# A decode step of gated attention and MLP: wo's extra rows loaded as one block, the biases of w1 and w2 applied elsewhere

## The chip, the cores and the metric

The kernel runs on one core of a Trainium2 chip. The metric is device time in microseconds (us) of one execution. A core has five engines that run in parallel: TensorE (PE; its weight loads are shown as PEld), VectorE (DVE), ScalarE (ACT), GpSimd (POOL) and SyncE (SP), which here issues nearly all loads. The loads themselves are carried out by 16 DMA engines, which work in parallel with all of these.

## What is computed

One token x (576 numbers, bf16) goes through two branches, and a gate mixes them:

```
g = sigmoid(sum(x * gate_w))
# branch a: attention of 32 query heads over 16 key/value heads,
#           the last 4096 positions of a cache, head size 128
q = x @ wq                                  # wq: 576 x 4096
p = softmax(q k^T / sqrt(128));  o = p v    # k, v: 16 x 4096 x 128 each
a = o @ wo                                  # wo: 4096 x 576
# branch b: MLP with a tanh gelu
b = gelu(x @ w1 + b1) @ w2 + b2             # w1: 576 x 4608, w2: 4608 x 576
out = g * a + (1 - g) * b
```

All inputs are bf16. About 53.6 MB must be read, 33.6 of them keys and values.

## The kernel before

**Stages.** SP issues the loads in one order: w1 (L234), wq (L238), the keys in four groups of four heads (L554, `k_t`), two groups of values, a third one, two small loads of wo (L670), the last group of values, the main part of wo (L771), the first half of w2 (L775) and the second half in four pieces of 10, 5, 2 and 1 rows per partition (L777). Big tiles share four buffers, named by the tags A to D: key group 2 goes where w1 was, group 3 where wq was, the values where keys were, wo and w2 last. A load therefore waits on SP until the last reader of its buffer is done. The small rows (x, the gate's weights, b2, b1) are loaded on ACT's queue at the start (L226 to L229).

**h stage.** x is put into a 32-column weight (`x2`). The function `moved` (L404) multiplies it with the nine rows per partition of w1: it takes the pieces four at a time, each of the four into another quarter of the output's partitions, and goes over five outputs (four of 512 columns, `h_m` of 256). Of the nine pieces, four and four fill two rounds. The ninth makes a third round together with b1, which is multiplied as two rows with a 2x32 corner of the identity, in the next quarter. A later product (L441) adds the four quarters up. A pass over the built program (`keep_weights`, L95) drops a weight load if the same weights still stand in that place and no weights of another size have been loaded between. ACT, POOL and DVE turn h into `gt`, the gelu with the factor (1 - g).

**q and attention.** wq is multiplied in the same way (L500). Then, by groups of four heads, DVE transposes the keys (L566), PE makes the scores (L588), DVE takes maxima, ACT exponentials, DVE transposes the probabilities, and PE multiplies them with the values (L681). A function `queue` keeps the instructions of an engine in the written order.

**Output stage.** wo has 128 rows for each of the 32 heads. The first 124 of a head are cut into 4 parts of 31 rows; the 32 x 4 parts fill the 128 partitions of `wo_t`. The four rows left of each head (124 to 127) are the extra rows, `wo_tail`: 32 heads, each 4 x 576 bf16 = 4,608 bytes. They lie in a part of the tile `zeros`, heads 0 to 15 in partitions 0 to 15 and heads 16 to 31 in partitions 32 to 47, and are loaded by two DMAs of 16 rows. A pass over the built program (`split_outer`, L74) gives each of these loads an outer dimension of 4:

```
ins=[copy.replace(src, ap=[[n // k * step, k], [step, n // k], [1, size]])],
outs=[copy.replace(dst, ap=[[part, n], [1, 1], [1, size]])],
```

The result y is accumulated in PSUM: `y_add` (L385) makes two products of 288 columns, the two halves of y, into partition 0 and partition 32 of `y_ps`. The first of these, L398, starts the sum early, with the row b2 x (1 - g) (`b2g`, L376) times 32 ones, so that partitions 0 to 31 and 32 to 63 all hold something. After attention come the four tail products (`ov_tail` times `wo_tail`), the 31 products with `wo_t`, and the first 23 rows of w2. A few fp32 products into a spare bank stand between (L831). DVE then copies `y_ps` to SBUF (`y_kept`, L844). The last 13 rows of w2 go into another pair of sums (`end_a`, `end_b`, L851); after the fifth of them, `y_carry` (L863) adds `y_kept` to these with a weight that picks rows 0 and 32. ACT and DVE cast the two parts (L879, L880), and SP stores them (L881).

The functions that the change touches:

Of the kernel before, what the change touches and what calls it, by code (L numbers as in the profile page):

```python
# [9 lines left out]
FP32 = mybir.dt.float32  # L10
BF16 = mybir.dt.bfloat16
I32 = mybir.dt.int32
ACT = mybir.ActivationFunctionType
ALU = mybir.AluOpType
# [4 lines left out]
def kernel(  # L19
# [15 lines left out]
    nc = tc.nc  # L35

    P = 128
    D = 576
    Hq, Hkv, Dh = 32, 16, 128
# [12 lines left out]
    DH = D // 2  # L52
# [19 lines left out]
    few_engines = {}  # L72
# [138 lines left out]
    const = ctx.enter_context(tc.tile_pool(name="const", bufs=1))  # L211
# [10 lines left out]
    b2_row = rows[0:1, 2 * D : 3 * D]  # L222
    b1_t = rows[0:2, 3 * D : 3 * D + FH]
# [21 lines left out]
    for base, pattern, keep in (  # L245
# [6 lines left out]
        n = 1  # L252
# [8 lines left out]
        out=is0[:], in0=low[:], scalar1=0.0, scalar2=None, op0=ALU.is_equal  # L261
    )
    alt = is0[:, 0 : 2 * NI].rearrange("p (i t) -> p i t", t=2)
    ones = const.tile([P, P], FP32, name="ones")
    nc.gpsimd.memset(ones[:], 1.0)
    ident = const.tile([P, P], BF16, name="ident")
    make_identity(nc, ident[:])
    RW = 31
    NZ = 5 * RW + 1 + 64
    ROWS = NZ + 4 * D  # L270
    zeros = const.tile([P, ROWS + 32 * HB], BF16, name="zeros")
    nc.gpsimd.memset(zeros[:].bitcast(FP32), 0.0)
    at31 = zeros[:, 0 : 5 * RW].rearrange("p (a r) -> p a r", a=5)
    om_t = zeros[:, NZ - 64 : NZ]
    wo_tail = zeros[0:48, NZ : NZ + 4 * D].rearrange("p (j n) -> p j n", j=4)
    nc.gpsimd.affine_select(
        out=at31,
        in_=at31,
# [8 lines left out]
        out=hi5[:],  # L287
        in_=ones[:, 0:5],
# [7 lines left out]
        out=hi5[:],  # L296
        in_=hi5[:],
# [9 lines left out]
        out=hi16[:], in0=is0[:, c0 : c0 + 16], scalar1=-SCALE, scalar2=None, op0=ALU.mult  # L307
# [6 lines left out]
        out=row_of,  # L314
        in_=row_of,
# [9 lines left out]
        out=foreign[:],  # L325
        in_=foreign[:],
# [11 lines left out]
        out=xdup.rearrange("p (d t) -> p d t", t=2),  # L338
        in_=x_row.rearrange("p (d o) -> p d o", o=1).to_broadcast([1, D, 2]),
    )  # L340
    xs_ps = ps_m.tile([P, NI, 1], FP32, name="xs_ps", tag="m")
    for i in range(NI):
        nc.tensor.matmul(  # L343
            xs_ps[:, i, :],
            lhsT=xdup[:, i : 2 * D : NI],
            rhs=ident[0:1, 0:1],
            start=(i == 0),
            stop=(i == NI - 1),
# [3 lines left out]
        out=x2[:, :, 0:2], in0=xs_ps[:].to_broadcast([P, NI, 2]), in1=alt, op=ALU.mult  # L352
# [5 lines left out]
        out=junk_row,  # L358
        in0=x_row,
        in1=gw_row,  # L360
        scale=1.0,
# [11 lines left out]
    nc.vector.reciprocal(out=g_t[:], in_=ge[:])  # L373
    omg = const.tile([P, 1], FP32, name="omg")
    nc.scalar.activation(out=omg[:], in_=g_t[:], func=ACT.Copy, scale=-1.0, bias=1.0)
    b2g = const.tile([1, D], FP32, name="b2g")  # L376
    nc.scalar.activation(out=b2g[:], in_=b2_row, func=ACT.Copy, scale=omg[0:1, 0:1])
    gh = const.tile([P, 1, 5], FP32, name="gh")
    nc.scalar.activation(out=gh[:, 0, :], in_=hi5[:], func=ACT.Copy, scale=g_t[:, 0:1])

# [1 line left out]
    y_ps = ps_y.tile([64, DH], FP32, name="y_ps")  # L382
    end_b = ps_y.tile([64, DH - DA], FP32, name="end_b")

    def y_add(vec, row, start=False, stop=False):  # L385
        wide = vec.shape[-1]
        for s in range(2):
            last = nc.tensor.matmul(  # L388
                y_ps[32 * s : 32 * s + wide, :],
                lhsT=vec,  # L390
                rhs=row[:, DH * s : DH * s + DH],
                start=start,
                stop=stop,
                skip_group_check=True,
            )
        return last

    y_add(ones[0:1, 0:32], b2g[0:1, :], start=True)  # L398


    QZ = 24
# [2 lines left out]
    def moved(pieces, last, start):  # L404
        for g0 in range(0, len(pieces), 4):
            for n in range(len(last)):
                for g in range(min(4, len(pieces) - g0)):
                    vec, part = pieces[g0 + g]
                    nc.tensor.matmul(  # L409
                        last[n][32 * g : 32 * g + 32],  # L410
                        lhsT=vec,
                        rhs=part(n),
                        start=start and g0 == 0,
                        stop=g0 + 4 + g >= len(pieces),
                        skip_group_check=True,
                    )
# [3 lines left out]
    h_out = [h_s[q // 2][:, 512 * (q % 2) : 512 * (q % 2) + 512] for q in range(4)]  # L420
    h_out.append(h_m[:])

    def columns(row):
        rows4 = row.rearrange("p (q l j) -> p q l j", q=4, j=NJ)
        return lambda n: rows4[:, n, :, 0:16] if n < 4 else rows4[:, :, :, 16:NJ]

    steps = [(x2[:, i, :], columns(w1_t[:, i, :])) for i in range(NI)]
    moved(steps[:4], h_out, True)
    moved(steps[4:] + [(ident[0:2, 0:32], columns(b1_t))], h_out, False)

    turned = kt_pool.tile([P, 2 * 1024 + 256], FP32, name="turned", tag="kt")
    for c0, src, q in ((0, h_s[0], 2), (1024, h_s[1], 2), (2048, h_m, 4)):
        n = 1024 if q == 2 else 256
        nc.vector.transpose(  # L434
            out=turned[:, c0 : c0 + n],
            in_=src[:].rearrange("p (q l j) -> p q j l", q=q, l=32),
# [3 lines left out]
    for j0, j1, b0 in ((0, 16, 0), (16, NJ, 64)):  # L440
        nc.tensor.matmul(  # L441
            hp_ps[:, :, :, j0:j1].rearrange("p q t j -> p q j t"),
            lhsT=same32,
            rhs=turned_t[:, b0 : b0 + 4 * (j1 - j0), :],
            start=(j0 == 0),
            stop=True,
# [3 lines left out]
    for q in range(4):  # L450
        quad = slice(32 * q, 32 * q + 32)
        nc.scalar.copy(
            out=hacc[quad], in_=hp_ps[quad, q, :, :].rearrange("p t j -> p (t j)")
# [6 lines left out]
        out=poly[:],  # L460
        in0=z2[:],
# [14 lines left out]
        out=gt[:], in0=hacc[:], scalar=omg[:, 0:1], in1=r_t[:], op0=ALU.mult, op1=ALU.mult  # L476
# [7 lines left out]
        out=pick[:],  # L484
        in_=pick[:],
# [16 lines left out]
    for c in range(2):  # L502
        nc.vector.transpose(  # L503
            out=q_turned[:, 1024 * c : 1024 * c + 1024],
            in_=q_s[c][:].rearrange("p (h l b) -> p h b l", l=32, b=2),
# [4 lines left out]
        lhsT=same32,  # L510
        rhs=q_turned[:].rearrange("p (h j l) -> p h j l", h=16, j=4)[:, :, :, 0:2],
        start=True,
        stop=True,
    )
    for b in range(4):
        quad = slice(32 * b, 32 * b + 32)
        at = QZ + 32 * b
# [4 lines left out]
            out=diag[:, :, :, 0:8],  # L522
            in_=qj_ps[quad].rearrange("p j g q -> p g j q"),
# [15 lines left out]
    o_ps = mt_ps[:, NG * 16 + Hq : NG * 16 + 2 * Hq]  # L539
    issued = {}  # L540

    def queue(engine, emit):
        if engine in issued:
            with tc.issue_after(issued[engine].ins):
                issued[engine] = emit()
        else:
            issued[engine] = emit()
# [117 lines left out]
    v_t = [load("v_t", "CD"[g], A_v_cache, g) for g in range(2)]  # L665
    v_t.append(load("v_t", "A", A_v_cache, 2))
    wo_src = A_wo.rearrange("(h d) n -> h d n", d=P)
    tail = wo_src[:, 4 * RW : P, :]
    for h0, h1, at, k in ((0, 16, 0, 4), (16, Hq, 32, 4)):
        load_tail = nc.sync.dma_start(  # L670
            out=wo_tail[at : at + h1 - h0].rearrange("h j n -> h (j n)"),
            in_=tail[h0:h1].rearrange("h j n -> h (j n)"),
        )
        few_engines[load_tail.ins.name] = k
    acc = [None] * NG
    summed = [None] * NG
    free_banks = []
# [35 lines left out]
    def outputs(g):  # L713
# [19 lines left out]
        out=ls[:],  # L733
        in0=same8[:, 0:8].rearrange("p (o q) -> p o q", o=1).to_broadcast([P, NG, 8]),
        in1=sums[:].to_broadcast([P, NG, 8]),
        op=ALU.mult,
# [11 lines left out]
            t_ps, lhsT=ones[:], rhs=ls[:].rearrange("p g q -> p (g q)"), start=True, stop=True  # L748
# [5 lines left out]
    rgh = const.tile([P, Hq, 5], FP32, name="rgh")  # L754
    nc.gpsimd.tensor_tensor(
        out=rgh[:],
        in0=rg[:].to_broadcast([P, Hq, 5]),
        in1=gh[:].to_broadcast([P, Hq, 5]),
        op=ALU.mult,
# [9 lines left out]
    RO = RW  # L769
    wo_t = big.tile([P, RO, D], BF16, name="wo_t", tag="D")  # L770
    nc.sync.dma_start(  # L771
        out=wo_t[:].rearrange("p r n -> p (r n)"),
        in_=wo_src[:, 0 : 4 * RW, :].rearrange("h (a r) n -> h a (r n)", a=4),
    )
    nc.sync.dma_start(out=w2_t[:, 0:NJ, :], in_=w2_src[:, 0])  # L775
    for j0, j1 in ((0, 10), (10, 15), (15, 17), (17, 18)):
# [5 lines left out]
    queue(  # L782
        "dve",
        lambda: nc.vector.tensor_tensor(
            out=om_t.rearrange("p (u h) -> p u h", u=2)[:, :, 0:16],
            in0=o_ps.rearrange("p (u h) -> p u h", u=2),
            in1=rgh[:, :, 4].rearrange("p (u h) -> p u h", u=2),
            op=ALU.mult,
        ),
    )  # L790
    queue(
# [2 lines left out]
            out=om[:], in0=o_all.to_broadcast([P, Hq, 4]), in1=rgh[:, :, 0:4], op=ALU.mult  # L794
# [3 lines left out]
    queue(  # L798
        "pe",
        lambda: nc.tensor.matmul(  # L800
            ov_ps[0:64, RO : RO + 4], lhsT=om_t, rhs=at31[:, 4, 0:4], start=True, stop=True
        ),
    )
    for a in range(4):
# [9 lines left out]
        )  # L814
    ov = const.tile([P, RO], BF16, name="ov")
    nc.vector.tensor_copy(out=ov[:], in_=ov_ps[:, 0:RO])
    ov_tail = const.tile([48, 4], BF16, name="ov_tail")
    nc.scalar.copy(out=ov_tail[:], in_=ov_ps[0:48, RO : RO + 4])

    late = [(ov_tail, j, wo_tail[:, j, :]) for j in range(4)]  # L820
    late += [512]
# [5 lines left out]
    for n, item in enumerate(late):  # L827
        if isinstance(item, int):
            queue(
                "pe",  # L830
                lambda: nc.tensor.matmul(  # L831
                    spare[:, 0:item],
                    lhsT=ones[:],
                    rhs=p_t[:].rearrange("p c k -> p (c k)").bitcast(FP32)[:, 0:item],
                    start=True,
                    stop=True,
                ),
            )
            continue
        vec, at, row = item  # L840
        queue("pe", lambda: y_add(vec[:, at : at + 1], row))

    y_kept = kt_pool.tile([33, DH], FP32, name="y_kept", tag="kt")
    nc.vector.tensor_copy(out=y_kept[:], in_=y_ps[0:33, :])  # L844
    end_a = ps_m.tile([64, DA], FP32, name="end_a", tag="m")
    ends = ((0, DA, end_a[0:2, :]), (DA, DH, end_b[32:34, :]))

# [64 lines left out]
```

## Time and profile before

| | us |
|---|---|
| median of three runs | 131.16 (130.96 to 131.59) |
| profiled execution | 131.3 |
| its span, first to last instruction | 130.0 |
| PE busy / share of the span | 79.6 / 61% |
| DVE busy / share | 61.3 / 47% |
| ACT, POOL busy | 11.4, 10.5 |
| chain that ended last: share of DMA, DVE, PE | 61%, 21%, 10% |
| bytes read from HBM, mean rate | 53.62 MB, 412 GB/s |

The page of the profile divides the span into 40 slices and gives each engine's busy share in tenths; the row DMA is the mean share of the 16 DMA engines. The chain that ended last is followed back from the last instruction, at each step to what released it. A timeline shows start and length of each instruction, with the tile it writes, the tiles it reads, and in brackets how long its engine was idle before it and what ended that. Besides, the trace holds one record for each DMA packet: queue, start, duration and size. A packet is one contiguous row of a load; packets of 4 bytes are the semaphore writes with which each DMA engine ends its share of a load.

### The profile page before, as it was taken

What the parts mean: (1) busy time and instruction counts of PE and PEld (TensorE: products, weight loads), DVE (VectorE), ACT (ScalarE), POOL (GpSimd) and SP (SyncE); (2) the same over time, 40 slices, a digit from 0 to 9 for tenths busy, and PEclk for the clock granted to TensorE, in tenths of its full rate; (3) what the DMA queues carried; (4) which work ended last, traced back from release to release, by engine and by line L of the source; (5) the groups of instructions that cost most, each with busy time, mean ns of one, the idle gap of its engine ahead of it and who ended that gap; (6) DMA issues with size and microseconds to landing.
All of it is one profiled execution on the core that took longest, in us unless ns stands there. A gap on an engine that the chain in (4) does not pass through costs nothing.

```text
span 130.0 us, 1210 instructions
## 1 busy us (share of the span) xinstructions
PE 79.6 (61%) x572; PEld 26.1 (20%) x442; DVE 61.3 (47%) x51; ACT 11.4 (9%) x27; POOL 10.5 (8%) x36
## 2 busy tenths in 40 slices
PE   0001499495007994859949945993374064789985
PEld 0001202200001120201212201140222021326553
DVE  0003104417099669999999994357705005100010
ACT  2130300210300000030003003012000000000000
POOL 7005940010000000000000000000100000000000
PEclk9999999959555899977999999599559558658999
DMA  8999899899899899799799899999999998999980
GB/s 255 499 460 421 364 420 488 353 474 474 353 464 474 338 474 474 333 484 484 343 464 484 373 433 484 403 403 479 378 433 444 427 461 373 459 394 427 412 328 29
DMA packets 2362, 53.69 MB, mean 413 GB/s; under 512 B 271, under 2 KB 404, under 8 KB 694
## 3 DMA queue, kind: packets, MB, share of 16 engines
q1 hardware_dynamic: 2348, 53.61, 96.6%
q8 instruction: 4, 0.07, 0.2%
q10 hardware_dynamic: 10, 0.01, 0.0%
HBM read 53.62 MB, written 0.00 MB: 412 GB/s over the span
## 4 chain that ended last, share of the span: by engine, by line
DMA 61%; DVE 21%; PE 10%; issue 5%; SPq 2%; DVEq 0%
DMA k_t<-in_A_k_cache_dram 34%; DMA w_t<-in_B_w_dram 26%; DVE kt L566 15%; PE s_ps L588 4%; DVE m L604 3%; DVE pt L637 2%; PE s_ps L681 1%; PE acc L681 1%; PE end_a L851 1%; SPq L775 1%; PE y_ps L388 1%; PE end_b L851 1%; PE mt_ps L613 1%; DVE mr L607 1%; SPq L554 0%
## 5 line engine op out<-in xcount | busy, mean ns | idle before, releaser
L588 PE MATMUL s_ps<-kt,qz_flat 128*128 128x512 bf16 x128 | 33.8, 423 | 13.1 <-DVE kt L566 9.4
L566 DVE STREAM_TRANSPOSE kt<-k_t 128x4096 f32<-128x4096 f32 x8 | 35.3, 4427 | 5.6 <-DMA k_t<-in_A_k_cache_dram 5.6
L588 PEld LDWEIGHTS <-qz_flat 128*128 128x128 bf16 x64 | 7.0, 109 | 37.2 <-issue 36.9
L681 PE MATMUL s_ps<-v_t,pt 128*32 128x512 bf16 x96 | 8.5, 518 | 7.0 <-DMA v_t<-in_A_v_cache_dram 7.0
L625 ACT ACTIVATE p_t<-s_ps,negm 128x1024 bf16<-128x1024 f32 x4 | 4.5, 1114 | 49.9 <-DVE negm L621 49.9
L695 DVE TENSOR_TENSOR own<-s_ps,is 128x512 f32<-128x512 f32 x3 | 2.1, 688 | 13.3 <-PE s_ps L681 13.3
L343 PE MATMUL xs_ps<-ident,rows 1*128 1x1 bf16 x9 | 0.6, 189 | 12.6 <-POOL ident masks.py:199 12.6
L844 DVE COPY y_kept<-y_ps 33x288 f32<-33x288 f32 x1 | 0.5, 450 | 14.4 <-PE y_ps L388 14.4
L681 PEld LDWEIGHTS <-pt 128*32 128x32 bf16 x128 | 3.7, 118 | 12.4 <-DMA v_t<-in_A_v_cache_dram 7.2
L637 DVE STREAM_TRANSPOSE pt<-p_t 128x1024 bf16<-128x1024 bf16 x4 | 4.9, 1224 | 2.7 <-ACT p_t L625 2.7
L604 DVE TENSOR_REDUCE m<-s_ps 128x1 f32<-128x1024 f32 x4 | 4.8, 1194 | 2.4 <-PE s_ps L588 2.4
L388 PE MATMUL y_ps<-wo_t,ov 128*1 128x288 bf16 x62 | 5.2, 342 | 0.5 <-DMA wo_t<-in_A_wo_dram 0.5
L357 DVE CUSTOM_DVE_ANT_0 rows<-rows 1x576 bf16<-1x576 bf16 x1 | 0.7, 746 | 10.1 <-DMA rows<-in_gate_w_dram 10.1
L716 PE MATMUL mt_ps<-is,summed 128*128 128x8 f32 x8 | 1.8, 293 | 6.0 <-DVE summed L705 6.0
L434 DVE STREAM_TRANSPOSE turned<-s_ps 128x1024 f32<-128x1024 f32 x2 | 2.5, 1250 | 6.1 <-PE s_ps L409 6.1
L409 PE MATMUL s_ps<-wq_t,x 128*32 128x512 bf16 x36 | 4.5, 576 | 1.2 <-DMA wq_t<-in_A_wq_dram 1.2
L732 POOL TENSOR_TENSOR ls<-is,sums 128x32 f32<-128x32 f32 x1 | 0.2, 243 | 60.8 <-ACT p_t L625 60.8
L409 PE MATMUL s_ps<-w_t,x 128*32 128x512 bf16 x36 | 4.9, 541 | 0.0
L705 DVE TENSOR_REDUCE summed<-own 128x128 f32<-128x512 f32 x4 | 4.1, 1020 | 0.1
L388 PEld LDWEIGHTS <-ov 128*1 128x1 bf16 x62 | 3.1, 98 | 3.9 <-issue 2.0
L831 PE MATMUL s_ps<-p_t,ones 128*128 128x512 f32 (+1 forms) x6 | 3.9, 738 | 0.0
L503 DVE STREAM_TRANSPOSE q_turned<-s_ps 128x1024 f32<-128x1024 f32 x2 | 2.4, 1228 | 2.3 <-PE s_ps L409 2.3
(95 smaller groups left out, 59.9 us busy)
## 6 DMA issues: line engine op xcount, KB each, us to landing
k_t<-in_A_k_cache_dram SPq DMA_DIRECT2D x4, 4096.0 KB, 40.1
v_t<-in_A_v_cache_dram SPq DMA_DIRECT2D x4, 4096.0 KB, 18.3
w_t<-in_B_w_dram SPq DMA_DIRECT2D x1, 5184.0 KB, 14.8
wq_t<-in_A_wq_dram SPq DMA_DIRECT2D x1, 4608.0 KB
wo_t<-in_A_wo_dram SPq DMA_DIRECT2D x1, 4464.0 KB
w_t<-in_B_w_dram SPq DMA_DIRECT2D x1, 2592.0 KB, 32.2
w_t<-in_B_w_dram SPq DMA_DIRECT2D x1, 1440.0 KB
w_t<-in_B_w_dram SPq DMA_DIRECT2D x1, 720.0 KB
```

The lines of the kernel that those rows point to most:

```text
L388: last = nc.tensor.matmul(y_ps[32 * s : 32 * s + wide, :], lhsT=vec, rhs=row[:, DH * s : DH * s + DH], start=start, stop=stop, skip_group_ ...
L409: nc.tensor.matmul(last[n][32 * g : 32 * g + 32], lhsT=vec, rhs=part(n), start=start and g0 == 0, stop=g0 + 4 + g >= len(pieces), skip_gro ...
L434: nc.vector.transpose(out=turned[:, c0 : c0 + n], in_=src[:].rearrange("p (q l j) -> p q j l", q=q, l=32),)
L566: lambda: nc.vector.transpose(out=kt[g, f][:].bitcast(FP32), in_=keys.rearrange("p c d -> p (c d)").bitcast(FP32),),
L588: last = nc.tensor.matmul(s_ps[g][:, u * 512 : (u + 1) * 512].rearrange("p (c k) -> p c k", k=32), lhsT=qz(g, j, 2 * f + half), rhs=kv[:, ...
L604: queue("dve", lambda: nc.vector.reduce_max(out=m1[:], in_=s_ps[g][:], axis=AX.X))
L625: nc.scalar.activation(out=p_t[:].rearrange("p c k -> p (c k)"), in_=s_ps[g][:], func=ACT.Exp, bias=negm[:, 0:1], scale=SCALE, accum_out=s ...
L637: lambda: nc.vector.transpose(out=pt[:, g, :, :].rearrange("p c q -> p (c q)"), in_=p_t[:].rearrange("p c k -> p (c k)"),),
L681: last = nc.tensor.matmul(acc[g][32 * (c % 4) : 32 * (c % 4) + 32, :], lhsT=pt[:, g, c, :], rhs=v_t[g][:, c:NCK:32, :], start=(c < 4), sto ...
L705: lambda: nc.vector.tensor_reduce(out=summed[g][:], in_=own[:].rearrange("p c d -> p d c"), axis=AX.X, op=ALU.add,),
L831: lambda: nc.tensor.matmul(spare[:, 0:item], lhsT=ones[:], rhs=p_t[:].rearrange("p c k -> p (c k)").bitcast(FP32)[:, 0:item], start=True, ...
L851: last = nc.tensor.matmul(to, lhsT=g_late[:, 2 * j + 1 - s : 2 * j + 3 - s], rhs=w2_t[:, NF - LATE + j, DH * s + c0 : DH * s + c1], start= ...
```

## The change

- The extra rows of wo are placed in partitions 0 to 31, in head order, and loaded by one DMA of 32 rows instead of two of 16. Its outer dimension is still 4. `om_t`, `ov_ps` and `ov_tail` get 32 columns or rows in place of 64 and 48.
- b1 is no longer in the same call of `moved` as w1's ninth piece, but in a call of its own, so that both use the first quarter, one after the other.
- `b2g` becomes a tile of 33 x 288 that POOL sets to zero; ACT writes the two halves of the scaled b2 to its rows 0 and 32. The product L398 that started `y_ps` is gone. DVE's copy of `y_ps` into `y_kept` becomes an addition of `y_ps` and `b2g`. The sum in `y_ps` is now started by the first tail product, whose one column is broadcast to 32.

```
-    NZ = 5 * RW + 1 + 64
+    NZ = 5 * RW + 1 + 32
...
-    om_t = zeros[:, NZ - 64 : NZ]
-    wo_tail = zeros[0:48, NZ : NZ + 4 * D].rearrange("p (j n) -> p j n", j=4)
+    om_t = zeros[:, NZ - 32 : NZ]
+    wo_tail = zeros[0:Hq, NZ : NZ + 4 * D].rearrange("p (j n) -> p j n", j=4)
...
-    b2g = const.tile([1, D], FP32, name="b2g")
-    nc.scalar.activation(out=b2g[:], in_=b2_row, func=ACT.Copy, scale=omg[0:1, 0:1])
+    b2g = const.tile([33, DH], FP32, name="b2g")
+    nc.gpsimd.memset(b2g[:], 0.0)
+    for s in range(2):
+        nc.scalar.activation(
+            out=b2g[32 * s : 32 * s + 1, :],
+            in_=b2_row[:, DH * s : DH * s + DH],
+            func=ACT.Copy,
+            scale=omg[0:1, 0:1],
+        )
...
-    y_add(ones[0:1, 0:32], b2g[0:1, :], start=True)
...
-    moved(steps[4:] + [(ident[0:2, 0:32], columns(b1_t))], h_out, False)
+    moved(steps[4:], h_out, False)
+    moved([(ident[0:2, 0:32], columns(b1_t))], h_out, False)
...
-    tail = wo_src[:, 4 * RW : P, :]
-    for h0, h1, at, k in ((0, 16, 0, 4), (16, Hq, 32, 4)):
-        load_tail = nc.sync.dma_start(
-            out=wo_tail[at : at + h1 - h0].rearrange("h j n -> h (j n)"),
-            in_=tail[h0:h1].rearrange("h j n -> h (j n)"),
-        )
-        few_engines[load_tail.ins.name] = k
+    load_tail = nc.sync.dma_start(
+        out=wo_tail.rearrange("h j n -> h (j n)"),
+        in_=wo_src[:, 4 * RW : P, :].rearrange("h j n -> h (j n)"),
+    )
+    few_engines[load_tail.ins.name] = 4
...
-            out=om_t.rearrange("p (u h) -> p u h", u=2)[:, :, 0:16],
-            in0=o_ps.rearrange("p (u h) -> p u h", u=2),
-            in1=rgh[:, :, 4].rearrange("p (u h) -> p u h", u=2),
-            op=ALU.mult,
+            out=om_t, in0=o_ps, in1=rgh[:, :, 4], op=ALU.mult
...
-            ov_ps[0:64, RO : RO + 4], lhsT=om_t, rhs=at31[:, 4, 0:4], start=True, stop=True
+            ov_ps[0:Hq, RO : RO + 4], lhsT=om_t, rhs=at31[:, 4, 0:4], start=True, stop=True
...
-    ov_tail = const.tile([48, 4], BF16, name="ov_tail")
-    nc.scalar.copy(out=ov_tail[:], in_=ov_ps[0:48, RO : RO + 4])
+    ov_tail = const.tile([Hq, 4], BF16, name="ov_tail")
+    nc.scalar.copy(out=ov_tail[:], in_=ov_ps[0:Hq, RO : RO + 4])
...
-        queue("pe", lambda: y_add(vec[:, at : at + 1], row))
+        column = vec[:, at : at + 1]
+        if n == 0:
+            column = column.to_broadcast([Hq, 32])
+        queue("pe", lambda: y_add(column, row, start=n == 0))
...
-    nc.vector.tensor_copy(out=y_kept[:], in_=y_ps[0:33, :])
+    nc.vector.tensor_tensor(out=y_kept[:], in0=y_ps[0:33, :], in1=b2g[:], op=ALU.add)
```

## The prediction

> **What bounds the kernel now.** I read the page's slices first. DMA and its GB/s stand high in every slice from start to end, while PE, DVE and ACT have empty ones. The queue table says the same: q1, the load queue, has packets in flight for 96.6% of 16 engines' time.
>
> ```profile
> PEclk9999999959555899977999999599559558658999
> DMA  8999899899899899799799899999999998999980
> q1 hardware_dynamic: 2348, 53.61, 96.6%
> q8 instruction: 4, 0.07, 0.2%
> ```
>
> Next the chain that ended last, in order of time, for what follows the last loads:
>
> ```profile
> 90.84 34.40 DMA w_t<-in_B_w_dram
> 125.24 0.04 issue
> 125.29 0.78 PE y_ps L388 x10
> ```
>
> Its columns are start, length and what. A load holds the chain to 125.24, and PE starts 0.05 us later. The packet records of the trace (start, duration, size and queue of every DMA packet) say why. The pieces of w2 whose packets are 11,520, 5,760, 2,304 and 1,152 bytes finish at 124.78, 126.52, 127.24 and 127.62; PE takes each up some 0.46 us later. What follows the last load is 2.4 us (127.62 to 130.0): the last four products, casts, the store. So the time is **when the slowest DMA engine ends its share, plus 2.4 us**.
>
> Those records chain into 16 streams without pauses (an engine's next packet starts 4 ns before the last one's end). To 125.4 all sixteen are busy; from 126 to 127 only about 7.5 are. Nine end near 125.8, seven between 127.0 and 127.6. What made seven late can be counted:
> - Four carry the two wo loads of the changed line. Their 32 packets of 4,608 bytes run from 92.96 to 94.98, and the chains show that *both* loads use the *same* four engines: four packets, a semaphore write, four more. That takes 1.59, 1.49, 1.66 and 1.68 us per engine. Eight packets one behind another at their usual 174 ns would be 1.39; some are stretched, to 389 ns at most.
> - Three others each carried one of q8's 16 KB instruction packets, at 44.48, 89.34 and 119.40 (0.93 to 1.08 us). A fourth comes at 126.68.
>
> **The change, part by part.** Sums are against the profiled execution, 131.3 us (span 130.0, 1.3 around it); the median of the runs shown is 131.16, so 0.1 comes off at the end. From no change, a measurement can tell about 0.5%, 0.66 us.
>
> *The second bias.* Before, four fp32 passes stand ahead of w1's products:
>
> ```profile
> 15.43 1.17 PE L388 MATMUL y_ps<-b2g,ones 1*32 1x288 f32 x4 [1.75 <-ACT b2g L377]
> 16.52 1.90 PE L409 MATMUL s_ps<-w_t,x 128*32 128x512 bf16 x16
> ```
>
> They go. x2 is ready at 15.21 and w1 landed at 14.48, so w1's products start near 15.3 instead of 16.52: 1.2 us. POOL gets a memset of 33x288 (estimated 0.33 us, between rows of 144 elements at 0.21 and 1084 at 0.99). ACT waits for it, then does two scalings of 288 in place of one of 576 at 0.76, about 0.2 us more in all. ACT's next work is at 24.65, and POOL's qz_flat, moved back 0.33, is read first at 32.80: both hidden.
>
> *w1's bias.* Now products with x and with the bias alternate, each with a new weight load:
>
> ```profile
> 20.26 0.38 PE L409 MATMUL s_ps<-rows,ident 2*32 2x512 bf16 x1
> 20.58 0.39 PE L409 MATMUL s_ps<-w_t,x 128*32 128x512 bf16 x1
> 20.90 0.39 PE L409 MATMUL s_ps<-rows,ident 2*32 2x512 bf16 x1
> ```
>
> Ten such steps of 0.32 us go from 19.93 to 23.18. In the built order after, five x products follow one weight load and five bias products another. At full clock sixteen L588 products of 512 columns take 3.63, so 0.227 each; eight of 512 and two of 256 make 2.05 us, 1.2 less. The h stage ends some 2.4 us earlier.
>
> What that buys: ACT's hacc and the load of k_t group 2, which SP held for h_m, are earlier. SP's wait:
>
> ```profile
> SPq L554 <- PE h_m L409: 8.3, 1, 8.3
> ```
>
> At 23.3, when that load is issued, wq still runs (to 25.4), and groups 0 and 1 of k stand behind it, up to 35 and 45. An earlier issue only lengthens the queue. wq's products wait for wq's landing (25.79) in both kernels; PE idles 2.4 us longer before them, and if the clock were low through all of their 4.45 us, the 4.5 us lost at most would fit in the 6 us between qz's copies (33.9) and the first scores (39.98). **Gain at the end: 0.**
>
> *The wo load.* One issue fewer (two cost SP 1.49 us at 78.51; SP's next issue is at 86.77, so nothing is behind it). Moving semaphores round, w2's fourth piece no longer waits for v (SP waited 3.2 us there, to 95) and the fifth does; their first packets move at 124.4 and 125.2: 0. Bytes are the same. If the split into four gives eight rows to the same four engines, each has the same eight packets, with one semaphore write (6 ns) less. What is not in the trace is whether eight packets into neighbouring rows cost what two fours, 32 rows apart, cost. Lower bound: 1.39 us without any stretching, 0.3 less than the slowest now. Upper bound: every packet at half pace, 2.78, which is 1.1 more than the 1.68 now. The nearest row is the two-row bias load early on: of its two 4,608-byte packets, at 6.28 and 14.11, the first is on another engine than the x row's, and both took 178 ns, with all the large packets around them at 1,533 to 1,535. No slowing shows, so I take **0**.
>
> *The end.* om_t stays 0.21, ov_ps and ov_tail shrink in width only, and the first tail products stay 288 columns long; all precede wo's landing at 115.21. y_kept turns from a copy into an add:
>
> ```profile
> 126.10 0.45 DVE L844 COPY y_kept<-y_ps 33x288 f32<-33x288 f32 x1 [14.37 <-PE y_ps L388]
> 126.64 0.09 PEld L863 LDWEIGHTS end_a<-y_kept,pick 33*2 33x2 f32 x2
> 126.99 1.24 PEld L851 LDWEIGHTS <-g_late 128*2 128x2 bf16 x32 [0.26 <-issue]
> ```
>
> TENSOR_TENSOR rows of 512 (0.69) and 32 (0.21) elements put 288 at 0.465: 0.015 more, and the products at 126.99 wait for a load (126.52 + 0.46) anyway.
>
> Sum: 0 to 0.02 on 131.3, so against the median **131.2 us**.
>
> **Rivals.**
> 1. *The four engines get slower* (the other side: slower). If the new places in SBUF make the tail packets share a way with other engines' streams, packets go at half pace: half of them adds 8/2 x 0.174 = 0.7, all adds 1.1. These engines never pause again, so a lag passes to the last landing one to one; it decides once their eight packets take over 2.3 us. For it: the last engine now is among these or close to them, and packets were stretched even before. Against it: the 178 ns row. The time: 131.9 to 132.4, say 132.2. [...]
> 2. *The program's code shifts.* PE's records before the four q8 packets number 183, 506, 768 and 952, on average 256 apart. After has 16 fewer early on (8 of the bias product, 8 weight loads), so each fetch comes later: the third by some 0.7 us, the fourth near 127.2, when a late engine still streams. It may put 0.3 on the last landing, or leave it 0.1 earlier (the next is 127.5). Should a fetch meet one of the four engines, 0.9 is added: 132.1.
> 3. *The saved PE time is worth its size*: 2.4 off, 128.8. Only if PE paced the loads; the DMA row without a gap speaks against it.
> 4. *The split isn't what it says*: the 32 rows on 16 engines, two each, add 0.36 to every engine and take 1.6 from four. The engines that fetch then end last, at 1.1 + 0.4: no change.
>
> **How the numbers follow.** Forecast with rival 4 and the small fetch shifts: 0.57, between 130.7 and 131.8. Rival 1: 0.32; rival 2's collision: 0.05; together slower by over 0.5%: 0.37. Rival 3, with any smaller gain of its kind: 0.06. The range 130.7 to 132.4 holds the forecast and most of rival 1, leaving out the rest.
>
> **What would show it.** Right: first products of w1 near 15.3, the h stage done near 20.8, k_t landings unchanged, the 4,608-byte packets over in about 2 us, and w2's last packet at 127.3 to 127.9. Rival 1: those packets spread over 2.5 to 3 us and the last landing as much later. Rival 3: earlier k_t landings. If the last landing stays while the time moves, the tail's 2.4 us were wrong.

## The result, and the profile after

The changed kernel takes **132.22 us** (median of 6 runs, 132.19 to 132.47); before takes 131.14 in the same comparison. The ratio is 1.0082, with a 95% interval of 1.0065 to 1.0098: slower by 0.8%. The forecast, no change, did not come true; the first rival did, at the time given for it.

First the same rows of the page as for before: the busy share of the 16 DMA engines in 40 slices, what they moved, and the load queue.

```profile
DMA  7999899999989999999998999999999998999981
GB/s 253 495 443 430 361 472 427 410 410 480 440 380 460 450 415 410 460 430 390 480 440 360 480 450 410 420 460 405 341 384 420 399 490 381 443 401 419 412 336 33
q1 hardware_dynamic: 2344, 53.61, 96.6%
```

The row of GB/s of before:

```profile
GB/s 255 499 460 421 364 420 488 353 474 474 353 464 474 338 474 474 333 484 484 343 464 484 373 433 484 403 403 479 378 433 444 427 461 373 459 394 427 412 328 29
```

The engines are as busy as before, 96.6% of a longer span, with the same bytes. Busy time tells nothing here; the row of GB/s gives a hint. Two slices side by side, 341 and 384, stand below their neighbours; they cover 92 to 98 us, where the extra rows of wo are loaded. Before has 378 and 433 there, and single slices down to 333 elsewhere, so a single low slice proves nothing. A table by stretches of time (columns: stretch, its length, TensorE's granted clock, DMA share, GB/s) puts it more clearly. A packet counts whole in the stretch in which it starts, so a share can come out a little over 1. Before:

```profile
core 0: us, , PEclk, DMA share, GB/s
84.00:92.00 8.00, 0.93 1.03 440
92.00:97.00 5.00, 0.50 1.01 423
97.00:120.00 23.00, 0.69 0.98 423
```

After:

```profile
core 0: us, , PEclk, DMA share, GB/s
84.00:92.00 8.00, 0.99 1.02 436
92.00:97.00 5.00, 0.50 1.01 331
97.00:120.00 23.00, 0.67 0.99 427
```

In five microseconds, (423 - 331) x 5 = 460 KB less arrive, at an unchanged busy share of 1.01. At 425 GB/s that is 1.08 us, the whole of the loss; on both sides of the stretch the rates agree within 1%. (A packet of 32 KB counts for 6.6 GB/s in such a stretch, so a difference of 20 is three packets at its edge.)

The end is the same chain as before, 1.1 us later:

```profile
88.38 37.98 DMA w_t<-in_B_w_dram
126.35 0.04 issue
126.40 0.78 PE y_ps L395 x10
```

The last packet of w2 ends at 128.73 instead of 127.62, and 2.4 us follow it in both (127.62 to 130.0; 128.73 to 131.1).

The packet records show where the time went. Below, *stretch* is the time by which the packets of the load queue that start between 92 and 96 us took longer than their usual time (1,213 ns for 32,768 bytes, 178 ns for 4,608), summed over 16 engines.

```
                  4,608-byte packets     mean ns   stretch, us   last packet of w2
before            92.96 to 94.98           203          1.7          127.62
after             92.89 to 95.84           280         19.3          128.73
```

(19.3 - 1.7) / 16 = 1.10 us for each engine. It isn't only the four engines with the extra rows that fall behind: chained into 16 streams as in the prediction, the records of after give each engine 1.1 to 1.3 us of stretch, and 25 packets of 32 KB that start between 92 and 97 us take from 1.4 to 2.2 us instead of 1.21, against two (1.43 and 1.47) in before.

### The profile page after: what moved, and what is told of

Read it like the earlier page. It is cut to its first block, busy times and chain, and to the rows that moved or that the text cites. A ratio compares the mean times of both kernels' runs of the same rounds, so it can differ in the third digit from the quotient of the medians.

```text
span 131.1 us, 1194 instructions
## 1 busy us (share of the span) xinstructions
PE 77.7 (59%) x568; PEld 25.0 (19%) x430; DVE 61.3 (47%) x51; ACT 11.8 (9%) x28; POOL 10.7 (8%) x37
## 3 DMA queue, kind: packets, MB, share of 16 engines
q1 hardware_dynamic: 2344, 53.61, 96.6%
## 4 chain that ended last, share of the span: by engine, by line
DMA 77%; DVE 11%; PE 8%; SPq 1%; issue 0%
DMA w_t<-in_B_w_dram 29%; DMA k_t<-in_A_k_cache_dram 26%; DMA v_t<-in_A_v_cache_dram 22%; DVE kt L573 10%; PE s_ps L595 4%; PE s_ps L686 1%; PE end_a L856 1%; DVE m L611 1%; PE y_ps L395 1%; PE end_b L856 1%; SPq L780 0%; SPq L776 0%; SPq L238 0%; DVE out_rows L885 0%; DVE mr L614 0%
## 5 line engine op out<-in xcount | busy, mean ns | idle before, releaser
L595 PE MATMUL s_ps<-kt,qz_flat 128*128 128x512 bf16 x128 | 32.5, 411 | 12.8 <-DVE kt L573 7.7
L343 PE MATMUL xs_ps<-ident,rows 1*128 1x1 bf16 x9 | 0.6, 189 | 12.7 <-POOL ident masks.py:199 12.7
L849 DVE TENSOR_TENSOR y_kept<-y_ps,b2g 33x288 f32<-33x288 f32 x1 | 0.5, 450 | 14.4 <-PE y_ps L395 14.4
L415 PE MATMUL s_ps<-wq_t,x 128*32 128x512 bf16 x36 | 5.0, 620 | 0.9 <-DMA wq_t<-in_A_wq_dram 0.9
```

What stands on the lines that cost most here:

```text
L415: nc.tensor.matmul(last[n][32 * g : 32 * g + 32], lhsT=vec, rhs=part(n), start=start and g0 == 0, stop=g0 + 4 + g >= len(pieces), skip_gro ...
L595: last = nc.tensor.matmul(s_ps[g][:, u * 512 : (u + 1) * 512].rearrange("p (c k) -> p c k", k=32), lhsT=qz(g, j, 2 * f + half), rhs=kv[:, ...
```

## The experiments

The theories at the outset. **Place:** packets are slow because of the partitions that they are written to. **Source:** they are slow because of the heads that are read at the same time, 4 apart in before and 8 apart in after; that all engines slow down seemed to speak for HBM.

**The biases alone, and the load alone.** The diff in two parts: `e1_biases` has the edits of `b2g`, `moved`, `y_add` and `y_kept`, `e2_load` those of `zeros`, `om_t`, `wo_tail`, `ov_ps`, `ov_tail` and the load.

> The two bias parts alone, with wo's extra rows loaded as before (two loads of 16 rows, partitions 0-15 and 32-47). All theories here blame the load, so this should give the time of before, 131.1 us within 0.3, with the large packets between 92 and 96 us stretched by under 3 us in sum over the 16 engines (1.7 in before, 19.3 in after). If it comes out near 132.2, the biases are the cause and the load is not.

> The load part alone: one load of 32 rows, biases as before. It should give the time of after, 132.2 us within 0.3, with some 19 us of stretch in sum between 92 and 96 us. If it gives 131.1 the load is innocent.

Measured: biases alone 131.13 us, ratio 1.0001 (0.9992 to 1.0010), stretch 0.5 us. Load alone 132.40 us, ratio 1.0089 (1.0068 to 1.0110), stretch 20.3 us. The load is the whole of it; both parts of the biases together cost nothing that the interval of 0.1% would show.

**Source or place.** `e3_two_loads_rows_0_31` is after with

```
-    load_tail = nc.sync.dma_start(
-        out=wo_tail.rearrange("h j n -> h (j n)"),
-        in_=wo_src[:, 4 * RW : P, :].rearrange("h j n -> h (j n)"),
-    )
-    few_engines[load_tail.ins.name] = 4
+    tail = wo_src[:, 4 * RW : P, :]
+    for h0, h1 in ((0, 16), (16, Hq)):
+        load_tail = nc.sync.dma_start(
+            out=wo_tail[h0:h1].rearrange("h j n -> h (j n)"),
+            in_=tail[h0:h1].rearrange("h j n -> h (j n)"),
+        )
+        few_engines[load_tail.ins.name] = 4
```

> After, but with two loads of 16 rows, so that each engine takes four heads, then four heads 16 further on, as in before; the places are those of after, partitions 0-31. Theory of the place (packets of two engines share a way into SBUF): slow, at least for the second load, 131.6 to 132.2 us. Theory of the source (what counts is which heads are read from HBM at the same time, 4 apart in before and 8 apart in after): the time of before, 131.1 us, and under 3 us of stretch.

`e4_heads_8_apart` is before with another order of the heads (and of `om_t`'s columns to match):

```
-                k = few_engines[i.name]
+                k, heads = few_engines[i.name]
...
-                    ins=[copy.replace(src, ap=[[n // k * step, k], [step, n // k], [1, size]])],
+                    ins=[copy.replace(src, ap=[[heads * step, k], [step, n // k], [1, size]])],
...
-    for h0, h1, at, k in ((0, 16, 0, 4), (16, Hq, 32, 4)):
+    for u, at in ((0, 0), (1, 32)):
...
-            in_=tail[h0:h1].rearrange("h j n -> h (j n)"),
+            in_=tail[4 * u : 4 * u + 16].rearrange("h j n -> h (j n)"),
...
-        few_engines[load_tail.ins.name] = k
+        few_engines[load_tail.ins.name] = (4, 8)
```

> Before, with its two loads and its places (partitions 0-15 and 32-47), but the heads dealt out as in after: the four engines read heads 0, 8, 16, 24 at the same time. Theory of the source: the time of after, about 132.2 us, with some 19 us of stretch. Theory of the place: the time of before, 131.1 us.

Measured: e3 131.90 us, ratio 1.0061 (1.0044 to 1.0079), stretch 12.7 us; e4 131.14 us, ratio 0.9999 (0.9989 to 1.0009), stretch 0.3 us. The theory of the source falls. The place counts. Two loads in place of one take back a part of the stretch at most (12.7 us against 19.3 and 20.3) and leave the kernel slow.

**Which places.** Are partitions 16 to 31 costly in themselves, whoever writes them (special rows), or does it depend on which engine writes where? The packet records name neither engine nor partition, so no trace shows which engine writes which partitions in the loads of 128 rows; the runs vary the number of engines and the rows. `e5_eight_engines` is after with one number changed:

```
-    few_engines[load_tail.ins.name] = 4
+    few_engines[load_tail.ins.name] = 8
```

> After, with the one load of 32 rows given an outer dimension of 8 in place of 4: eight engines take four neighbouring rows each, in the same partitions 0-31. [...] Theory of special rows (partitions 16 to 31 are costly, whoever writes them): stretch of 10 us or more and 131.7 us or more.

`e6_rows_48_63` and `e7_rows_64_79` are before with `(16, Hq, 32, 4)` turned into `(16, Hq, 48, 4)` and `(16, Hq, 64, 4)`, and `om_t`, `wo_tail`, `ov_ps` and `ov_tail` made as wide as that needs.

> Before, with the second load of 16 rows put in partitions 48-63 instead of 32-47. [...] Special rows: 131.1 us, no stretch.

> [...] Special rows: 131.1 us.

`e8_sixteen_engines` is after with 16 in that line. That the load is split as written shows in the load queue's packet count: 2,344 in after, 2,348 in e5 and 2,356 in e8, that is, one closing semaphore write for each of 4, 8 and 16 engines.

> After, with an outer dimension of 16: all engines take two rows each, in partitions 0-31. [...]

The same stretch of time, first in e5:

```profile
core 0: us, , PEclk, DMA share, GB/s
84.00:92.00 8.00, 1.00 1.05 449
92.00:97.00 5.00, 0.64 0.94 403
```

and in e7:

```profile
core 0: us, , PEclk, DMA share, GB/s
84.00:92.00 8.00, 0.96 1.02 436
92.00:97.00 5.00, 0.50 0.98 351
97.00:120.00 23.00, 0.60 1.00 428
```

e7 loses 72 GB/s there with rows far from 16 to 31. e5's 403 comes with a share of 0.94 in place of 1.01: 423 x 0.94 / 1.01 = 394, so its packets are not slower, there are fewer in the stretch. The packet records say it without that doubt:

```
                       us       ratio (95%)                 stretch, us
e5  rows 0-31, k = 8   131.50   1.0024 (1.0014 to 1.0033)       0.4
e6  0-15, 48-63        131.96   1.0064 (1.0049 to 1.0080)      14.4
e7  0-15, 64-79        131.85   1.0058 (1.0044 to 1.0072)      13.4
e8  rows 0-31, k = 16  132.29   1.0089 (1.0075 to 1.0103)      13.5
```

The special rows fall: the same 32 neighbouring rows, in one load, have 0.4 us of stretch as soon as eight engines take four each, where 10 us or more were forecast, and e6 and e7 take 131.96 and 131.85 us with 14.4 and 13.4 us of stretch, where 131.1 us was. More engines are not the remedy in themselves: with sixteen (e8) the stretch is 13.5 us.

**Moved by four rows.** `e9_shifted_both` moves both loads of before up by four partitions (`(0, 16, 4, 4), (16, Hq, 36, 4)`), `e10_shifted_second` only the second (`(0, 16, 0, 4), (16, Hq, 36, 4)`).

> [...]

> [...]

Measured: e10 is at 131.33 us, ratio 1.0010 (0.9999 to 1.0021), stretch 2.6 us, against 13 to 14 in e6 and e7, which also differ from before in the places of the second load alone. Only two packets of 32 KB take over 1.4 us there (1,580 and 1,699 ns, both from 94.27); by the chains, one is on an engine that has just ended its extra rows and the other on an engine that has none. e9 is at 132.01 us, ratio 1.0057 (1.0041 to 1.0074), stretch 9.3 us, half of after's 19.3. Its second load lies where e10's does, so the move of the first adds 6.7 us of stretch; what sets the size of that stays open.

**Without the extra rows.** `e12_no_tail` is before without the loop of the two loads.

> Before, without the two loads of wo's extra rows (that part of wo is left out of the result). If the lag of the four engines passes to the end one to one as long as they are last, the end falls back to the engines that carried an instruction packet, which lag about 1.1 us where the four lag 1.5 to 1.7: 130.5 to 130.9 us. If the extra rows are hidden, 131.1.

Measured: 131.04 us against 131.25 in that comparison, ratio 0.9986 (0.9973 to 0.9998). Loaded to the places of before, the rows cost 0.2 us (0.03 to 0.35), less than a lag passed on one to one would give (130.5 to 130.9 us were forecast for that). A single profile doesn't resolve it: w2's last packet ends at 127.40 here and at 127.62 in before, but also at 127.36 in e1, which loads the rows.

## Why the prediction failed, point by point

The measured 132.22 us lies in the stated range of 130.7 to 132.4, but only because that range was drawn to hold most of rival 1. The forecast itself, 131.2 us within 130.7 to 131.8, missed.

*What bounds the kernel.* This held. The loads set the end, and the last landing plus 2.4 us gives the time in both kernels.

*The second bias.* Its pieces came as forecast: w1's products start at 15.40 (15.3 was said), the memset takes 0.33 us (0.33), the two scalings 1.08 us in all where 0.96 was worked out, and none of it shows at the end (e1).

*w1's bias.* PE's timeline of after, with start and length:

```profile
17.32 1.90 PE L415 MATMUL s_ps<-w_t,x 128*32 128x512 bf16 x16
...
19.24 1.51 PE L415 MATMUL s_ps<-w_t,x 128*32 128x512 bf16 x4
20.59 0.39 PE L415 MATMUL h_m<-w_t,x 128*32 128x256 bf16 x1
20.91 1.03 PE L415 MATMUL s_ps<-rows,ident 2*32 2x512 bf16 x4
21.78 0.39 PE L415 MATMUL h_m<-rows,ident 2*32 2x256 bf16 x1
```

The stage ends at 22.2, 1.0 us earlier than before and not 2.4. The row used for its price, L588 with 0.227 us a product, did not apply, although the granted clock was 1.00 from 15 to 23 us in both kernels. The five x products take 1.67 us (19.24 to 20.91), 0.33 each, as much as a step of the alternating products did; the five with the bias take 1.26. Together that is 2.93 us in place of 3.25, a saving of 0.3 and not 1.2. The second round, counted between the starts of the rows of `h_m`, took 1.92 us (17.08 to 19.00) where before's took 1.51 (18.20 to 19.71); the runs don't say why. These errors had no effect, since the stage is hidden, as e1 shows.

*The end.* The addition takes what the copy took, 0.45 us (0.015 more was forecast):

```profile
127.22 0.45 DVE L849 TENSOR_TENSOR y_kept<-y_ps,b2g 33x288 f32<-33x288 f32 x1 [14.43 <-PE y_ps L395]
127.76 0.08 PEld L868 LDWEIGHTS end_a<-y_kept,pick 33*2 33x2 f32 x2
```

*Rival 2, the code.* In after the instruction packets come at 48.00, 89.26, 120.43 and 129.18, where they came at 44.48, 89.34, 119.40 and 126.68. In e1, which has all of after's changes to the bias products, they come at 48.03, 89.41, 119.38 and 127.88, and the time is that of before. The third isn't later by the 0.7 us that was worked out, and the fourth is later than the 127.2 that was. No effect on the time shows.

*Rivals 3 and 4.* Both fall. In e1 the h stage ends at 21.99 in place of 23.18, and the time is that of before. The split is what it says, as the packet counts above show.

*The wo load: the step that failed.* It was "No slowing shows, so I take 0"; the term measured 1.1 us. The nearest row was a single packet of 4,608 bytes, early on, which took 178 ns. One packet could not bear the conclusion for 32, and the prediction itself gave rival 1, slower packets, a chance of 0.32. The step's two bounds, besides, were only about the eight packets on each of the four engines. The cost fell on all sixteen, 1.1 to 1.3 us of stretch on each, and no term of the sum had that.

*Rival 1* had the cause, the new places, and the time, 132.2, but its sum was right by luck. It let the four engines run their eight packets at half pace and kept the twelve others whole. No run shows the half pace, nor that the packets share a way with other streams. In fact these packets took 280 ns on average instead of 203, (280 - 203) x 8 = 0.6 us for each of the four, and the loss was spread: 1.1 us on each of the sixteen. With only the four behind by 0.6 us, the end should have moved by less; no run isolates that.

Of the places the runs show this. With four engines, rows 0-15 with 32-47 are cheap (1.7 us of stretch in before, 0.5 in e1, 0.3 in e4). Rows 0-31 are not (19.3 in after, 20.3 in e2, 12.7 in e3), nor are 0-15 with 48-63 (14.4, e6) or with 64-79 (13.4, e7). With four rows on each of eight engines, rows 0-31 have 0.4 us (e5). Why a place is cheap for some engines and dear for others, and why in after all sixteen lose about the same, 1.1 to 1.3 us each, the runs here don't say.

Open, besides that: why e5, without stretch, is still 0.24% above before. In the slow runs with four engines, the stretch divided by 16 gives the loss within 0.2 us (e2: 1.27 worked out, 1.28 measured; e6: 0.90, 0.88). In e5 and e8, which put the rows on 8 and 16 engines, the loss is 0.4 us more (0.02 and 0.42; 0.84 and 1.21), so the rest seems to go with the number of engines and not with the place; no run tests that. Also open is whether one load into the places of before would be as good as two, which was not tried. None of the variants is faster than before by more than the 0.14% that leaving the rows out gives, so none is a better kernel.

## What to carry to other kernels

When loads set the time, a load of few rows is not only its bytes: ask how many engines carry it and which partitions they write, and measure another split and other places. Here four neighbouring rows on each of eight engines (e5), or two fours 32 rows apart on each of four (before), caused no stretch to speak of (0.4 and 1.7 us). Rows 0-31 on four engines, rows 48-63 or 64-79 in place of 32-47, both loads moved by four rows, and two rows on each of sixteen engines cost 0.6 to 0.9%; only the second load moved by four rows (e10) cost nothing clear of noise. Look for such a loss in GB/s by stretches of time, never in the busy share, which was 1.01 in both kernels while the packets took longer.

## What the runs showed of the hardware that was not expected

- The 32 packets of 4,608 bytes (147 KB) slowed the streams of all 16 engines in after, by 1.1 to 1.3 us each. That took some 4 us (92.8 to 97.2), and packets of 32,768 bytes took up to 2,204 ns instead of 1,213. In the places of before as many such packets gave 1.7 us of stretch over all 16.
- A single such packet, with the rows of b1 at 6.28 us, slowed nothing: the packets of 41,472 bytes around it took 1,533 to 1,535 ns. The second load moved by four rows (e10) gave 2.6 us of stretch over 16 engines, which the time does not show (ratio 1.0010, 0.9999 to 1.0021).
